# Linear attention and a Fourier mix on one core: loads as two streams, one pool of eight PSUM banks, the division in six operations, and a changed rank

## The chip, the cores and the metric

The kernel runs on one core of one Trainium2 chip. The metric is the device time of one execution in microseconds (us). Runs of the same kernel are compared on the same chip.

The core's engines run side by side, each in the order of its own instruction list. TensorE (PE; its weight loads are listed as PEld) multiplies matrices and transposes, and writes to PSUM, which has eight banks of 128 x 512 float32. VectorE (DVE) and ScalarE (ACT) read PSUM and compute elementwise. GpSimd (POOL) computes elementwise in SBUF, the on-chip memory, and issues the weights' DMAs. SyncE (SP) issues all other DMAs, in order: one that waits holds up those behind it.

## What is computed

The inputs are q, k and v of 8 batches x 8 heads x 576 rows x 64, a matrix omega of 128 x 64, and two weight matrices, 512 x 2048 and 2048 x 512. All is float32.

```python
q_s, k_s = (q * scale, k * scale)
def phi(x):
    proj = np.einsum('bhsd,md->bhsm', x, omega)
    sq = np.sum(x * x, axis=-1, keepdims=True) / 2.0
    h = proj - sq
    h = h - np.max(h, axis=-1, keepdims=True)
    return np.exp(h) / np.sqrt(m)
q_p, k_p = (phi(q_s), phi(k_s))
kv = np.einsum('bhsm,bhsd->bhmd', k_p, v)
z = np.sum(k_p, axis=2)
num = np.einsum('bhsm,bhmd->bhsd', q_p, kv)
den = np.einsum('bhsm,bhm->bhs', q_p, z)[..., None] + 1e-06
x = num / den                       # heads side by side: 8 x 576 x 512
...
X = np.fft.fft(x, axis=1)
X = np.fft.fft(X, axis=2)
u = x + np.real(X).astype(np.float32)
mu = np.mean(u, axis=-1, keepdims=True)
var = np.mean((u - mu) ** 2, axis=-1, keepdims=True)
un = (u - mu) / np.sqrt(var + 1e-06)
ch = np.maximum(un @ w_ch1, 0.0) @ w_ch2
return u + ch
```

## The kernel before

**Attention** goes over 32 pairs of heads, four to a batch. `loads()` (L241) fetches k and q of a pair into one kq tile (288 KB each, L248 and L251) and v into one of the fixed vd buffers (two DMAs of 144 KB, L254); vd has a column of ones per head, so that the product with it gives the sum z as well. `attn(n)` (L404) works on one pair: nine transposes of kq (tps, L368), evicted by ACT to kqT; products with omega (pp, L429), in five groups of at most 512 columns; the negated maximum on DVE (nmx, L384) and the exponential on ACT (e, L396); the product of k's features with vd (kvp, L451), kept by DVE as kv (L463); transposes of q's features (tps, L368) to qeT; and 18 products of qeT with kv, nine for each head (ndp, L493), into two banks. Each of these 18 gives 64 rows, and `SLOTS` (L28) says in which half of the partitions and in which of five slots of 65 columns a product lands. PE lists two instructions for each such product. The last step (L498 to L513) adds a small number to the denominators, inverts them and multiplies, and writes x: three DVE operations for each head on the four slots with 128 rows, and three on the fifth slot, which has 64 rows: twelve in all.

**Mixing** (`mix`, L520) works on a batch when its four pairs are done: folds on DVE, products with tables of cosines and sines on PE (yp L572, ab L599 and L604), and sums; u then goes to DRAM (us, uh). The tables are loaded within `loads()`, behind the second pair's v (L258).

**The weights** come as float64 (`weights`, L318): POOL loads 32 raw pieces of 512 KB into four slab buffers, and ACT, DVE and POOL narrow each to float32 (`narrow`, L297).

**The network behind it** has two forms. Four plain tiles of 128 rows (`plain_of`, L748: hp L780, evicted to ht; op L803; residual ur L816) are computed beside attention. The other 4096 rows come as eight blocks of 512, whose products are taken by halves (sx, sy, sz; L934 and L1024), after attention is over. A tile is normed by `norm_of` (L700): u is loaded from DRAM into one of two u buffers, normed on DVE (L709 to L715), transposed on PE (tp, L719) and evicted to unT. The first block's norms (`block_norms(0, mlpp)`, L832) are also listed beside attention, once all weights are narrowed; the four slab buffers then hold them.

**What sets the order.** No engine chooses its work while the kernel runs. Every piece of work is a `Step` with an engine, a cost, a due time `late` that is added to its end before others may use what it made, the events it needs (`after`), and the buffers it takes and gives back. `Listing.run` (L88) always takes, of the next steps of all streams, the one that could begin earliest; between equal ones that of the stream that stands earlier in the list goes first, and this is what rank means here. Each engine's list is written in this order. A `Step` is only a plan: what really waits on the chip is what its data and buffers demand.

The streams before stand in this order: `first`, `loads`, `frames` (which hands out the two x buffers), `plain_norms`, `mixing`, three streams `pairs` that each run every third pair, `plain`, `weights`, and the first block's norms. There are three kq buffers, two vd buffers, six PSUM banks for all of attention, mixing and norms (`bank`), and two that only the plain tiles use (`mm`).

Of the kernel before, what the change touches and what calls it, by code (L numbers as in the profile page):

```python
# [14 lines left out]
ALU = mybir.AluOpType  # L15
# [147 lines left out]
def kernel(  # L163
# [10 lines left out]
    nc = tc.nc  # L174
# [16 lines left out]
    R = S // 64  # L191

    NS = 3
    NV = 2
    NKQ = 3
    NE = 7


# [30 lines left out]
    buffers = dict(  # L229
        bank=6, mm=2, kq=NKQ, turned=NS, e=NE, e1=NS, kv=NS, x0=1, x1=1, fold=1, half=1, y=1,  # L230
        bmp=2, slab=4, u=2, unT=1, ht=NFC, ur=1, **{f"vd{i}": 1 for i in range(NV)},
    )

# [7 lines left out]
    def loads():  # L241
        for n in range(B * NP):
            b, pr = divmod(n, NP)
            h = slice(2 * pr, 2 * pr + 2)
            rows = "i (p r) d -> (i p) r d"
            yield Step(SP, 0.5, 3.0, take=("kq",))
            kq = ld.tile([P, 2 * R, D], F32, name="kq", tag="kq")
            nc.sync.dma_start(kq[:, 0:R, :], k[b, h].rearrange(rows, r=R))  # L248
            kqs[n] = kq
            yield Step(SP, 0.45, 4.0, makes=("kq", n))  # L250
            nc.sync.dma_start(kq[:, R : 2 * R, :], q[b, h].rearrange(rows, r=R))  # L251
            yield Step(SP, 1.3, 4.5, take=(f"vd{n % NV}",), makes=("vd", n))
            for i in range(2):
                nc.sync.dma_start(  # L254
                    vds[n % NV][D * i : D * i + D, :, (D + 1) * i : (D + 1) * i + D],
                    v[b, 2 * pr + i].rearrange("(p r) d -> p r d", r=R),
                )
# [145 lines left out]

    def attn(n):  # L404
        b, pr = divmod(n, NP)
        yield Step(NONE, after=(("kq", n), "om2"))
        kq = kqs.pop(n)

        flat = kq[:].rearrange("p c d -> p (c d)")
# [75 lines left out]
        )  # L485
        ndp = [bank("ndp"), bank("ndp")]

        for i, order in enumerate(((0, 2, 1, 4, 3, 7, 8, 5, 6), (2, 1, 4, 3, 7, 8, 5, 6, 0))):
            for r in order:
                g, slot = SLOTS[r]  # L490

                c0 = D * (1 - i if r >= 5 else i)
                nc.tensor.matmul(  # L493
                    ndp[i][D * g : D * g + D, (D + 1) * slot : (D + 1) * slot + D + 1],
                    lhsT=qeT[:, r, c0 : c0 + D],
                    rhs=kvs[0][:, i, :],
                )
        yield Step(DVE, 2.0, after=(("frame", b),), give=("bank", "bank"), makes=("x", b, pr))  # L498
        x = xts[b % 2]
        rden = small.tile([P, 2, 5], F32, name="rden", tag="rden")  # L500
        for i in range(2):
            nd = ndp[i][:, 0 : 5 * (D + 1)].rearrange("p (c d) -> p c d", d=D + 1)
            cols = slice((2 * pr + i) * D, (2 * pr + i + 1) * D)
            for p1, c0, c1 in ((P, 0, 4), (64, 4, 5)):
                den = rden[0:p1, i, c0:c1]
                nc.vector.tensor_scalar(den, nd[0:p1, c0:c1, D], DEN_EPS, None, op0=ALU.add)
                nc.vector.reciprocal(out=den, in_=den)
                nc.vector.tensor_tensor(
                    out=x[0:p1, c0:c1, cols],
                    in0=nd[0:p1, c0:c1, 0:D],  # L510
                    in1=den.unsqueeze(2).to_broadcast([p1, c1 - c0, D]),
                    op=ALU.mult,
                )  # L513

    def frames():
        for b in range(B):
# [231 lines left out]
    def plain_of(j):  # L748
# [4 lines left out]
        def hidden(fc, hp):  # L753
            step = Step(
                {ACT: 0.15 + TP / 1130.0, DVE: 0.15 + TP / 945.0},
                late=0.1,
                take=("ht",),
                give=("mm",),
                makes=("ht", key, fc),
            )  # L760
            yield step
            ht = mlpp.tile([128, TP], F32, name="ht", tag="ht", bufs=NFC)
            if step.eng == DVE:
                nc.vector.tensor_scalar(ht[:], hp[:, 0:TP], 0.0, None, op0=ALU.max)
            else:
                nc.scalar.activation(out=ht[:], in_=hp[:, 0:TP], func=AF.Relu)
            hs[fc] = ht

        for fc in range(NFC):
            yield Step(  # L770
                PE,
                8 * TP / 1193.0,
                after=tuple(("unT", key, i) for i in range(nt))
                + tuple(("w", fc * 128 // CV * NDC + dc) for dc in range(NDC)),
                take=("mm",),
                give=("unT",) if fc == NFC - 1 else (),
            )
            hp = mmp.tile([128, 512], F32, name="hp", tag="mm")
            for dc in range(NDC):
                nc.tensor.matmul(  # L780
                    hp[:, 0:TP],
                    lhsT=w1[:, dc, 128 * fc : 128 * fc + 128],
                    rhs=unTs[key][:, dc, :],
                    start=(dc == 0),
                    stop=(dc == NDC - 1),
                )
            yield Fork(hidden(fc, hp))
        for i in range(nt):
            for f0 in range(0, NFC, 2):
                yield Step(  # L790
                    PE,
                    1.72,
                    after=tuple(("ht", key, f) for f in (f0, f0 + 1))
                    + tuple(("w", NDC * DFF // CV + f) for f in (f0, f0 + 1)),
                    take=("mm",) if f0 == 0 else (),
                    give=("ht", "ht") if i == nt - 1 else (),
                    makes=("op", nt * j + i) if f0 == NFC - 2 else None,
                )
                if f0 == 0:
                    yp = mmp.tile([128, DM], F32, name="op", tag="mm")  # L800
                    yield Fork(rest(nt * j + i, yp))
                for fc in range(f0, f0 + 2):
                    nc.tensor.matmul(  # L803
                        yp[:],
                        lhsT=hs[fc][:, 128 * i : 128 * i + 128],
                        rhs=w2[:, fc, :],
                        start=(fc == 0),
                        stop=(fc == NFC - 1),
                    )

    def rest(t, yp):
        yield Step(SP, 0.5, 2.7, take=("ur",))
        ur = mlpp.tile([P, DM], F32, name="ur", tag="ur", bufs=1)
        load_rows(ur, t)
        yield Step(DVE, 0.7, after=(("op", t),), give=("mm",))
# [39 lines left out]
    def pairs(start):  # L855
# [268 lines left out]
```

## Time and profile before

| | us |
|---|---|
| median of three runs | 1384.61 |
| lowest and highest | 1383.97, 1388.35 |
| the profiled execution | 1387.42 |
| its span, first to last instruction | 1385.7 |

The profiled execution is 1.7 us longer than its span, and 2.8 us longer than the median. In the timelines a line gives the start, the length, the engine and line of the kernel, the operation, output and inputs, and in square brackets how long the engine had been idle before it and what ended that. The lists of waits give, for each pair of waiter and releaser, the total in us, the number of times, and the longest. A matmul's length is that of one instruction through the pipeline; several are under way at once, so what they cost is read from the distance of their starts.

### The profile page before, as it was taken

The numbers are of one execution on the slowest core, as the hardware profiler recorded it, in microseconds if no ns is written. First come the engines' busy times: TensorE is split into PE (matmuls) and PEld (weight loads), VectorE is DVE, ScalarE is ACT, GpSimd is POOL, SyncE is SP. The second block draws the span as 40 slices with busy tenths as digits, with TensorE's granted clock in tenths as the row PEclk, the third lists the DMA queues.
The fourth block names the chain that finished last, engine by engine and source line by source line (L and its number), as shares of the span: only waits on it lengthen the run. The fifth ranks groups of instructions, "written<-read, shape, count | busy, mean of one in ns | idle before, by whom it ended". The sixth has DMA issues, their size and how long they took to land.

```text
span 1385.7 us, 20262 instructions
## 1 busy us (share of the span) xinstructions
PE 1317.3 (95%) x7777; PEld 1137.5 (82%) x7777; DVE 586.7 (42%) x1545; ACT 409.1 (30%) x1194; POOL 291.8 (21%) x404
## 2 busy tenths in 40 slices
PE   6897989798999999889999999999999999999998
PEld 5777888676898786678888888888888888888887
DVE  2686878876666554155123123113123122132111
ACT  4664564555465451121021021020120120110210
POOL 1213123221100000034033042042140140330330
PEclk8999999999999999999999999999999999999999
DMA  7516155624422321110020100200200200200101
GB/s 193 153 43 192 53 169 169 173 90 114 124 78 77 79 88 37 37 54 16 14 63 16 46 31 16 76 1 16 76 0 16 76 7 13 73 16 8 54 1 31
DMA packets 82465, 89.67 MB, mean 65 GB/s; under 512 B 42944, under 2 KB 51392, under 8 KB 82368
## 3 DMA queue, kind: packets, MB, share of 16 engines
q1 hardware_dynamic: 77760, 71.59, 19.0%
q0 software_dynamic: 4608, 16.78, 3.7%
q8 instruction: 62, 1.02, 0.3%
q14 instruction: 35, 0.29, 0.1%
HBM read 69.47 MB, written 23.07 MB: 67 GB/s over the span
## 4 chain that ended last, share of the span: by engine, by line
PE 85%; DMA 6%; DVE 4%; SPq 2%; issue 1%; ACT 1%; POOL 1%; DVEq 0%; ACTq 0%; POOLq 0%
PE sx L1024 16%; PE sx L934 16%; PE sz L1024 8%; PE sz L934 8%; PE pp L429 7%; PE sy L1024 4%; PE hp L780 4%; PE sy L934 4%; PE yp L572 4%; PE op L803 4%; PE tps L368 3%; PE kvp L451 3%; PE ndp L493 2%; DMA kq<-in_q_dram 2%; PE ab L599 2%; DMA kq<-in_k_dram 2%
## 5 line engine op out<-in xcount | busy, mean ns | idle before, releaser
L396 ACT ACTIVATE e<-pp,nmx 128x128 f32<-128x128 f32 x576 | 156.7, 413 | 63.1 <-DVE nmx L384 61.6
L998 POOL TENSOR_TENSOR hs<-ht,ht 128x256 f32<-128x256 f32 x64 | 47.9, 750 | 488.5 <-DVE ht L921 488.5
L948 ACT ACTIVATE s<-sx 128x256 f32<-128x256 f32 x128 | 48.9, 383 | 344.0 <-PE sx L934 326.7
L429 PE MATMUL pp<-om,kqT 128*128 128x256 f32 x576 | 140.7, 391 | 1.1 <-ACT kqT L375 1.1
L934 PE MATMUL sx<-unT,w 128*128 128x256 f32 x512 | 131.2, 379 | 0.8 <-DVE ur L816 0.8
L429 PEld LDWEIGHTS pp<-om,kqT 128*128 128x128 f32 x576 | 108.7, 196 | 20.5 <-issue 2.0
L384 DVE TENSOR_REDUCE nmx<-pp 128x4 f32<-128x512 f32 (+1 forms) x160 | 96.0, 630 | 63.0 <-PE pp L429 59.1
L1024 PE MATMUL sx<-w,ht 128*128 128x256 f32 x512 | 114.4, 379 | 0.0
L934 PEld LDWEIGHTS sx<-unT,w 128*128 128x128 f32 x512 | 97.2, 190 | 14.8 <-DVE ur L816 1.6
L1024 PEld LDWEIGHTS sx<-w,ht 128*128 128x128 f32 x512 | 96.7, 190 | 12.9
L921 DVE CUSTOM_DVE_ANT_0 ht<-sz,s 128x256 f32<-128x256 f32 x64 | 27.1, 425 | 184.7 <-PE sz L934 184.7
L316 POOL TENSOR_TENSOR w<-w,raw 128x512 f32<-128x512 f32 x32 | 45.4, 1424 | 195.0 <-DVE raw L314 194.8
L1035 DVE TENSOR_TENSOR ur<-ur,sx 128x256 f32<-128x256 f32 x64 | 26.9, 421 | 139.8 <-PE sx L1024 139.8
L451 PE MATMUL kvp<-vd,e 128*128 128x130 f32 x576 | 75.3, 281 | 10.9 <-DMA vd<-in_v_dram 9.4
L451 PEld LDWEIGHTS kvp<-vd,e 128*128 128x128 f32 x576 | 71.7, 195 | 16.9 <-issue 10.8
L368 PE MATMUL tps<-ident,kq 128*128 128x128 f32 x288 | 49.1, 308 | 32.8 <-DMA kq<-in_k_dram 27.0
L981 ACT ACTIVATE ht<-sx 128x256 f32<-128x256 f32 x64 | 24.5, 383 | 172.3 <-PE sx L934 172.3
L368 PEld LDWEIGHTS tps<-ident,kq 128*128 128x128 f32 x288 | 37.3, 157 | 40.8 <-issue 28.8
L375 ACT ACTIVATE kqT<-tps 128x512 f32<-128x512 f32 (+1 forms) x96 | 43.7, 497 | 82.1 <-PE tps L368 81.8
L934 PE MATMUL sz<-tt,w1s 128*128 128x256 f32 x256 | 65.6, 379 | 1.9 <-DVE w1s L906 1.9
L934 PE MATMUL sx<-tt,w 128*128 128x256 f32 x256 | 65.6, 379 | 1.0 <-DVE ht L921 1.0
L934 PE MATMUL sz<-unT,w1s 128*128 128x256 f32 x256 | 65.5, 379 | 0.0
(105 smaller groups left out, 2329.5 us busy)
## 6 DMA issues: line engine op xcount, KB each, us to landing
raw<-in_moe_w_ch_dram POOLq DMA_DIRECT2D x32, 512.0 KB, 6.6
kq<-in_k_dram SPq DMA_DIRECT2D x32, 288.0 KB, 5.1
kq<-in_q_dram SPq DMA_DIRECT2D x32, 288.0 KB, 5.1
vd<-in_v_dram SPq DMA_DIRECT2D x64, 144.0 KB, 4.4
out_dram<-ur SPq DMA_DIRECT2D x72, 128.0 KB, 2.4
u<-us SPq DMA_DIRECT2D x32, 256.0 KB, 3.8
ur<-us SPq DMA_DIRECT2D x32, 256.0 KB, 3.6
uh<-x SPq DMA_DIRECT2D x16, 256.0 KB, 2.0
```

Of the source, the lines that this page charges most:

```text
L368: nc.tensor.transpose(ps[:, (j - j0) * 128 : (j - j0 + 1) * 128], src(j), ident[:])
L384: nc.vector.tensor_reduce(nmx[:, 0:num], ps[:, 0 : MF * num].rearrange("p (c m) -> p c m", m=MF), axis=AX.X, op=ALU.max, negate=True,)
L396: nc.scalar.activation(out=e[:, c, :], in_=ps[:, MF * c : MF * c + MF], func=AF.Exp, bias=nmx[:, c : c + 1],)
L429: nc.tensor.matmul(ps[:, 256 * j : 256 * j + 256], lhsT=kqT[:, 2 * t + j, :], rhs=om2[:].rearrange("p i m -> p (i m)"),)
L451: nc.tensor.matmul(kvp[:, 0 : 2 * (D + 1)], lhsT=feature(r), rhs=vds[n % NV][:, r, :], start=(r == 0), stop=(r == R - 1),)
L572: nc.tensor.matmul(yp[:, 0:NK], lhsT=fold[:, c, n, :], rhs=tab[:, c, :], start=(c == 0), stop=(c == NC3 - 1),)
L780: nc.tensor.matmul(hp[:, 0:TP], lhsT=w1[:, dc, 128 * fc : 128 * fc + 128], rhs=unTs[key][:, dc, :], start=(dc == 0), stop=(dc == NDC - 1),)
L803: nc.tensor.matmul(yp[:], lhsT=hs[fc][:, 128 * i : 128 * i + 128], rhs=w2[:, fc, :], start=(fc == 0), stop=(fc == NFC - 1),)
L934: nc.tensor.matmul(ps[:, 0:HT], lhsT=left(dc), rhs=right(dc), start=start and dc == 0, stop=(dc == D2 - 1), skip_group_check=True,)
L948: nc.scalar.activation(out=s[:], in_=ps[:, 0:HT], func=AF.Copy)
L998: nc.gpsimd.tensor_tensor(out=o, in0=l, in1=r, op=op)
L1024: nc.tensor.matmul(ps[:, 0:HM], lhsT=left(fc), rhs=right(fc), start=start and fc == 0, stop=(fc == HF - 1), skip_group_check=True,)
```

## The change

- The loads become two streams. `loads()` keeps k and q, with due times of 5.0 and 5.5 us, and the tables behind the second q; the new `loads_v()` stands right behind it in the list and has v. There are three vd buffers instead of two, and two kq buffers instead of three.
- A pair's stream now also waits, in the plan, for the v of the pair before.
- The pools of six and two PSUM banks become one of eight, from which the plain tiles take too.
- The products for r = 0 leave their slots: for each head one product with a stationary operand of 128 columns instead of 64 is written to a slot of its own in the second bank (only its first 64 rows are used), so that this bank holds six slots and the first four. The last step on DVE is then two additions, one inversion of all ten columns, and three multiplications. Its planned cost is 1.8 us instead of 2.0.
- The first block's norms stand ahead of `plain` and `weights` in the list of streams.

```diff
-    NV = 2
-    NKQ = 3
+    NV = 3
+    NKQ = 2
...
-    psum = early.enter_context(tc.tile_pool(name="psum", bufs=6, space=PSUM))
-    mmp = early.enter_context(tc.tile_pool(name="mmp", bufs=2, space=PSUM))
+    psum = early.enter_context(tc.tile_pool(name="psum", bufs=8, space=PSUM))
...
-            yield Step(SP, 0.5, 3.0, take=("kq",))
+            yield Step(SP, 0.6, 5.0, take=("kq",))
...
-            yield Step(SP, 0.45, 4.0, makes=("kq", n))
+            yield Step(SP, 0.45, 5.5, makes=("kq", n))
             nc.sync.dma_start(kq[:, R : 2 * R, :], q[b, h].rearrange(rows, r=R))
-            yield Step(SP, 1.3, 4.5, take=(f"vd{n % NV}",), makes=("vd", n))
+            if n == 1:
+                yield from load_tables()
+
+    def loads_v():
+        for n in range(B * NP):
+            b, pr = divmod(n, NP)
+            yield Step(SP, 1.3, 5.5, take=(f"vd{n % NV}",), makes=("vd", n))
             for i in range(2):
...
-            if n == 1:
-                yield from load_tables()
...
-        yield Step(NONE, after=(("kq", n), "om2"))
+        yield Step(NONE, after=(("kq", n), "om2") + ((("vd", n - 1),) if n else ()))
...
-        for i, order in enumerate(((0, 2, 1, 4, 3, 7, 8, 5, 6), (2, 1, 4, 3, 7, 8, 5, 6, 0))):
+        for i, order in enumerate(((2, 1, 4, 3, 7, 8, 5, 6), (2, 1, 4, 3, 7, 8, 5, 6))):
...
+        flat = qeT[:].rearrange("q c p -> q (c p)")
+        for i in range(2):
+            nc.tensor.matmul(
+                ndp[1][:, (D + 1) * (4 + i) : (D + 1) * (5 + i)],
+                lhsT=flat[:, D * i : D * i + P],
+                rhs=kvs[0][:, i, :],
+            )
...
-        for i in range(2):
-            nd = ndp[i][:, 0 : 5 * (D + 1)].rearrange("p (c d) -> p c d", d=D + 1)
-            cols = slice((2 * pr + i) * D, (2 * pr + i + 1) * D)
-            for p1, c0, c1 in ((P, 0, 4), (64, 4, 5)):
-                den = rden[0:p1, i, c0:c1]
-                nc.vector.tensor_scalar(den, nd[0:p1, c0:c1, D], DEN_EPS, None, op0=ALU.add)
-                nc.vector.reciprocal(out=den, in_=den)
-                nc.vector.tensor_tensor(
...
+        for i, n in enumerate((4, 6)):
+            nc.vector.tensor_scalar(
+                rden[:, 4 * i : 4 * i + n], nds[i][:, :, D], DEN_EPS, None, op0=ALU.add
+            )
+        nc.vector.reciprocal(out=rden[:], in_=rden[:])
+        cols = x[:, :, 2 * D * pr : 2 * D * (pr + 1)].rearrange("p c (i d) -> p c i d", i=2)
+        for p1, dst, nd, den in (
+            (P, cols[:, 0:4, 0], nds[0], rden[:, 0:4]),
+            (P, cols[:, 0:4, 1], nds[1][:, 0:4], rden[:, 4:8]),
+            (64, cols[0:64, 4], nds[1][0:64, 4:6], rden[0:64, 8:10]),
+        ):
+            nc.vector.tensor_tensor(
...
-            hp = mmp.tile([128, 512], F32, name="hp", tag="mm")
+            hp = bank("hp")
...
-                    yp = mmp.tile([128, DM], F32, name="op", tag="mm")
+                    yp = bank("op")
...
-        [first(), loads(), frames(), plain_norms(), mixing()]
+        [first(), loads(), loads_v(), frames(), plain_norms(), mixing()]
         + [pairs(i) for i in range(NS)]
-        + [plain(), weights(), block_norms(0, mlpp)]
+        + [block_norms(0, mlpp), plain(), weights()]
```

More of the change, by code (lines that the diff above doesn't have):

```diff
@@ L497, in attn @@
                 )
-        yield Step(DVE, 2.0, after=(("frame", b),), give=("bank", "bank"), makes=("x", b, pr))
-        x = xts[b % 2]
-        rden = small.tile([P, 2, 5], F32, name="rden", tag="rden")
-        for i in range(2):
-            nd = ndp[i][:, 0 : 5 * (D + 1)].rearrange("p (c d) -> p c d", d=D + 1)
-            cols = slice((2 * pr + i) * D, (2 * pr + i + 1) * D)
-            for p1, c0, c1 in ((P, 0, 4), (64, 4, 5)):
-                den = rden[0:p1, i, c0:c1]
[L506 to L513, printed above, removed]
+        flat = qeT[:].rearrange("q c p -> q (c p)")
[5 more added lines that the diff above has]
+            )
+        yield Step(DVE, 1.8, after=(("frame", b),), give=("bank", "bank"), makes=("x", b, pr))
+        x = xts[b % 2]
+        rden = small.tile([P, 10], F32, name="rden", tag="rden")
+        nds = [
+            t[:, 0 : (D + 1) * n].rearrange("p (c d) -> p c d", d=D + 1)
+            for t, n in zip(ndp, (4, 6))
+        ]
+        for i, n in enumerate((4, 6)):
[10 more added lines that the diff above has]
+            nc.vector.tensor_tensor(
+                out=dst,
+                in0=nd[:, :, 0:D],
+                in1=den.unsqueeze(2).to_broadcast(list(dst.shape)),
+                op=ALU.mult,
+            )
     def frames():
@@ L757, in hidden @@
                 take=("ht",),
-                give=("mm",),
+                give=("bank",),
                 makes=("ht", key, fc),
@@ L774, in plain_of @@
                 + tuple(("w", fc * 128 // CV * NDC + dc) for dc in range(NDC)),
[L775 removed]
+                take=("bank",),
                 give=("unT",) if fc == NFC - 1 else (),
             )
[L778 removed]
+            hp = bank("hp")
             for dc in range(NDC):
@@ L794, in plain_of @@
                     + tuple(("w", NDC * DFF // CV + f) for f in (f0, f0 + 1)),
-                    take=("mm",) if f0 == 0 else (),
+                    take=("bank",) if f0 == 0 else (),
                     give=("ht", "ht") if i == nt - 1 else (),
@@ L814, in rest @@
         load_rows(ur, t)
-        yield Step(DVE, 0.7, after=(("op", t),), give=("mm",))
+        yield Step(DVE, 0.7, after=(("op", t),), give=("bank",))
         nc.vector.tensor_tensor(out=ur[:], in0=ur[:], in1=yp[:], op=ALU.add)
```

6 lines of the change are left out of this document (3 added, 3 removed).

## The prediction

> **What bounds the kernel now.** I read the page's busy line first, then the span cut in two where the halved blocks begin, then TensorE's waits.
>
> ```profile
> PE 1317.3 (95%) x7777; PEld 1137.5 (82%) x7777; DVE 586.7 (42%) x1545; ACT 409.1 (30%) x1194; POOL 291.8 (21%) x404
> ```
>
> ```profile
> 0.00:591.48 591.48, 530.68 (x4082) 445.89 (x4082) 377.40 (x1069) 294.44 (x910) 94.94 (x120) 0.97 0.39 109
> 591.48:1385.70 794.22, 786.61 (x3696) 691.64 (x3696) 209.34 (x476) 114.66 (x284) 196.91 (x284) 1.00 0.12 31
> ```
>
> The columns of the second view are the stretch, its length, and the busy time of PE, PEld, DVE, ACT and POOL; then the granted clock, the DMA share and GB/s. In the halved blocks PE stands for 7.6 us, so nothing is to be had there, and the change does not touch their instructions. In the first 591 us it stands for 60.8 us, and the clock averages 0.97. PE is the bound there too, so a gain must come out of those 60.8 us, the clock, or PE's work. What PE waits for:
>
> ```profile
> PE tps L368 <- DMA kq<-in_k_dram: 27.0, 8, 8.6
> PE kvp L451 <- DMA vd<-in_v_dram: 9.4, 4, 5.2
> PE tp L719 <- DVE u L715: 5.7, 1, 5.7
> ```
>
> Loads make 36.4 of the 60.8 us. One of them in time, on SP's queue and on PE:
>
> ```profile
> 60.35 0.97 SPq L248 DMA_DIRECT2D kq<-in_k_dram  x1
> 61.37 0.43 SPq L251 DMA_DIRECT2D kq<-in_q_dram  x1
> 63.43 1.55 SPq L254 DMA_DIRECT2D vd<-in_v_dram  x2
> 65.03 0.65 SPq L248 DMA_DIRECT2D kq<-in_k_dram  x1
> 65.72 0.43 SPq L251 DMA_DIRECT2D kq<-in_q_dram  x1
> 108.22 1.22 SPq L254 DMA_DIRECT2D vd<-in_v_dram  x2
> ```
>
> ```profile
> 63.24 0.71 PE L368 MATMUL tps<-ident,e 128*128 128x128 f32 x5
> 68.28 0.63 PE L368 MATMUL tps<-ident,kq 128*128 128x128 f32 x4 [4.33 <-DMA kq<-in_k_dram]
> ...
> 325.27 2.16 PE L368 MATMUL tps<-ident,kq 128*128 128x128 f32 x9 [2.40 <-DMA kq<-in_k_dram]
> ```
>
> ```profile
> DMA to landing us min/median/max: 3.2/5.1/9.7
> ```
>
> A pair's v waits for one of two vd buffers, at 108.22 for 42 us, and the next pair's k and q stand behind it in the one list of `loads()`. When the buffers come free, three pairs' loads leave together and PE, which runs in order, reaches the transposes of k before k has landed (the last row: the 32 loads of k, median 5.1, longest 9.7 us). Each such stand costs twice, since the granted clock then drops:
>
> ```profile
> 69.80:73.20 3.40, 3.38 (x14) 3.16 (x15) 0.00 (x0) 1.96 (x5) 0.00 (x0) 0.57 0.26 74
> ...
> 325.80:329.20 3.40, 3.40 (x44) 2.89 (x42) 0.39 (x3) 1.36 (x3) 0.00 (x0) 0.57 0.81 264
> sum 20.40, PE 19.02 PEld 17.69 DVE 6.26 ACT 11.79 POOL 4.12; mean PE 3.80 PEld 3.54 DVE 1.25 ACT 2.36 POOL 0.82
> ```
>
> These are the first and last of five stretches behind load waits, with their sum: 19.02 us of PE at a clock of 0.54 to 0.57, so about 0.45 of it, 8.6 us, is lost.
>
> The Trainium skill, TensorE: Matmul & The Clock Gate, Part 1, says that the array falls to half rate after an idle window of about 3.4 us. The row at 325.27 shows a wait of 2.40 us with the clock at 0.57 right behind it, so here shorter waits cost clock as well; by the page's rule alone such short waits cost no clock, the 2.2 us of clock that I leave over below would go as well, and the time would be 1358.
>
> **The change part by part.**
>
> *Loads in two streams.* k and q no longer stand behind v: with two kq buffers they leave when the pair two ahead has been transposed, and v, with three, when the kvp three ahead is done. In the code the due times become 5.0 and 5.5 us for k and q instead of 3.0 and 4.0, near the measured median of 5.1, and a pair starts only when the v before its own is due; so the written order puts other PE work where PE now stands. At stake after the start: 27.0 - 8.6 (the longest, at 23.83, taken with the start below) = 18.4, plus 9.4 for v = 27.8 us, and 8.6 of clock. Bounds: all of it goes (-36.4) or none. Loads up to 9.7 us remain longer than their due times, so I take three quarters: -20.9 and -6.4. The added waits sit in SP's one queue: behind a k that waits for transposes stand stores of us and out, loads of u and ur, and v. Those are the price if PE is late, and are the rivals below.
>
> *The start.* The tables are yielded inside `loads()` behind the second q, so they now go ahead of the first v.
>
> ```profile
> 6.58 1.26 SPq L291 DMA_DIRECT2D cs_sb<-k_cs  x2
> ...
> 16.00 2.89 SPq L291 DMA_DIRECT2D sd_sb<-k_sd  x2
> 20.02 0.35 SPq L248 DMA_DIRECT2D kq<-in_k_dram  x1
> ```
>
> ```profile
> 11.12 2.17 PE L451 MATMUL kvp<-vd,e 128*128 128x130 f32 x18
> ...
> 14.66 0.60 PE L368 MATMUL tps<-ident,e 128*128 128x128 f32 x4
> 23.83 1.09 PE L368 MATMUL tps<-ident,kq 128*128 128x128 f32 x4 [8.57 <-DMA kq<-in_k_dram]
> ```
>
> What follows the tables in the queue now, the third k, lands at 23.8. The first v takes that place less the v loads that no longer precede it, so at 20 to 24 instead of before 11.1: PE stands about 11 us from 11.1 instead of 8.6 us from 15.3. Behind it the first two pairs' work covers the third k. Cost 2.5 us; bounds -5 (the v lands by 15) to +6.
>
> *Eight banks in one pool.* No row shows PE waiting for a bank by name. It lets attention use two more banks, and lets the plain tiles take more than two. I take nothing, bounds -5 to +6.
>
> *The first block's norms rank higher.* Now they go last:
>
> ```profile
> 505.48 0.54 DVE L715 TENSOR_SCALAR u<-u,mv,rstd 128x512 f32<-128x512 f32 x1
> ```
>
> ```profile
> 552.20 1.04 PE L719 MATMUL tp<-ident,u 128*128 128x128 f32 x8
> 558.92 1.11 PE L719 MATMUL tp<-ident,u 128*128 128x128 f32 x4 [5.68 <-DVE u L715]
> ```
>
> ```profile
> 557.90:564.70 6.80, 5.09 (x24) 4.69 (x25) 0.55 (x1) 1.08 (x3) 0.39 (x1) 0.53 0.33 100
> ```
>
> A normed u is ready at 506 and is transposed at 552; it holds a u buffer, and the last plain tile's norm can only begin then, so PE stands 5.7 us and then works 5.09 us at 0.53 (2.4 lost). Ranked ahead of the plain tiles the transposes come early and that buffer is free. -8.1, bounds -8.1 to 0.
>
> *The last step, on DVE.* Twelve operations become six.
>
> ```profile
> L506 DVE TENSOR_SCALAR rden<-ndp x128: 140/143/163, 30.0 to 522.6; 128x4 f32<-128x4 f32 x64, 64x1 f32<-64x1 f32 x64
> L507 DVE RECIPROCAL rden<-rden x128: 154/168/181, 30.2 to 522.8; 128x4 f32<-128x4 f32 x64, 64x1 f32<-64x1 f32 x64
> L508 DVE TENSOR_TENSOR x<-ndp,rden x128: 216/321/426, 30.4 to 523.0; 128x256 f32<-128x256 f32 x64, 64x64 f32<-64x64 f32 x64
> ```
>
> Before, 4 x (0.143 + 0.168 + 0.321) = 2.53 us a pair. After, 2 x 0.143 + 0.168 + three products, two of 0.426 and one of 64x128 between 0.216 and 0.426: 1.6 to 1.7. About 0.85 a pair, 27 us over 32 pairs, but DVE is busy for 377 of 591 us and PE covers it. I take nothing; bounds -7 (a quarter reaches the path) to 0.
>
> *The same step, on PE.* It keeps its 36 instructions a pair (two for each product), but the four for r = 0 now use the array's whole width instead of half of it.
>
> ```profile
> 45.66 2.55 PE L493 MATMUL ndp<-kv,qeT 128*64 128x65 f32 x72
> 48.14 0.70 PE L429 MATMUL pp<-om,kqT 128*128 128x256 f32 x2
> ```
>
> ```profile
> 102.48 0.73 PE L604 MATMUL ab<-mid,cs_sb 128*128 128x1 f32 x6
> 103.07 0.69 PE L599 MATMUL ab<-cd_sb,y 128*128 128x129 f32 x4
> ```
>
> Half-width ones start (48.14 - 45.66) / 72 = 34 ns apart, whole ones with hardly any columns (103.07 - 102.48) / 6 = 98 ns. 4 x 0.064 x 32 = +8.2 us of PE work. Bounds 0 to 8.2; I take the upper, as PE is the bound and 98 ns is the nearest row.
>
> The Trainium skill, TensorEngine Tiling (Array Packing), Key Properties, says that tiles of a split array load and multiply in parallel; that speaks against this part. By it a whole-width product costs what two packed ones cost, +0.034 each, 4.4 us in all, and the sum would be 3.8 lower; the rows say 98 against 34, so I keep 8.2.
>
> **Sum**, against the profiled execution's 1387.4 (span 1385.7): +2.5 - 20.9 - 6.4 - 8.1 + 8.2 = -24.7, so 1362.7. That execution lies 2.8 above the median of 1384.6, so 1360.
>
> **The rivals.**
>
> *The wait moves (0.19).* Two streams are still one in-order queue: if a k stands behind a v or a store as often as now, the 18.4 us stay with their share of the clock (5.7). Only v's part goes: +2.5 - 7.1 - 2.2 - 8.1 + 8.2 = -6.7, that is 1378. For it: SP's order is written from due times that the long loads exceed. Against it: a k needs only transposes, which come first in a pair, where now it needs a v buffer, which comes free late.
>
> *Two kq buffers are too few (0.14), slower.* Three pairs run at once, so of each three the last's k can leave only when the first's transposes are done. If the three are transposed in a row, PE does the second's nine (four took 0.63, so about 1.3 us) and stands for the rest of a landing between 5.1 and 9.7, say 7.4 - 1.3 = 6.1, with 1.7 of clock (8.6 over five stretches): 7.8 for each of ten such groups. Seven of ten make 54.6 against the 36.4 that go: +18.2 + 2.5 - 8.1 + 8.2 = +20.8, or 1405. It decides from (36.4 - 2.6) / 7.8, about five groups of ten. Against it: the due times now carry 5.0 us, so the list would have to be wrong by some 2 us each time.
>
> *DVE was on the path (0.10).* Then 7 us more go: 1353.
>
> **How the numbers follow.** The forecast holds 0.57 and spans 1345 to 1376 by its own bounds. Measurement tells some 0.3% (4 us) from no change: faster is all of the forecast but 0.02, DVE's 0.10 and half of the moved wait (0.10), 0.75; the rest of the moved wait and of the forecast is 0.11; slower 0.14. Down, all of the load waits, clock and tail go and the start gains 5: 1338. Up, the range takes in the moved wait and the near end of the slower rival: 1390.
>
> **What would show it.** Loads: the waits of tps on k after 30 us under 8 us, and the clock at 1.0 through the stretches above. Start: kvp at 20 to 24 with about 11 us idle before it, on v. Norms: the block's transposes before 500 and no 5.7 us wait near the end. PE: the whole-width products 90 to 100 ns apart. Most of the gain must lie before the first halved block, which should begin some 25 us earlier. Wrong would be: the k waits of the same size at other places, waits of pp on banks that a plain tile holds, or halved blocks that take other than 794 us.

## The result, and the profile after

The change took the median from 1386.09 to 1330.17 us; the ratio is 0.960, with a 95% interval of 0.958 to 0.963. That is 56 us, where 25 were forecast, and below the range. The profiled execution took 1329.8 us, 57.7 less than the one before. The first product of the halved blocks starts at 533.95 instead of 591.48 us, so all of it lies ahead of them. First the stretches up to and from there, in the view by windows with the columns of before:

```profile
0.00:533.95 533.95, 516.00 (x4081) 443.14 (x4081) 348.95 (x871) 292.43 (x916) 97.57 (x123) 0.99 0.43 121
533.95:1328.00 794.05, 786.62 (x3696) 692.13 (x3696) 209.16 (x476) 114.67 (x284) 196.71 (x284) 1.00 0.12 31
```

The halved blocks are what they were (794 us). Before them PE stands for 18.0 us instead of 60.8, and it is busy for 14.7 us less. Cut once more, at 40 us, behind the start; first the kernel before, then the change:

```profile
0.00:40.00 40.00, 27.16 (x176) 23.76 (x177) 14.18 (x36) 21.62 (x65) 6.56 (x20) 0.87 0.69 183
40.00:591.48 551.48, 503.52 (x3908) 422.13 (x3906) 363.22 (x1034) 272.82 (x846) 88.39 (x100) 0.97 0.36 104
```

```profile
0.00:40.00 40.00, 26.11 (x163) 23.13 (x164) 15.32 (x33) 20.51 (x62) 9.66 (x25) 0.87 0.83 217
40.00:533.95 493.95, 489.88 (x3920) 420.01 (x3918) 333.64 (x839) 271.93 (x856) 87.92 (x98) 1.00 0.40 113
```

After the first 40 us PE's idle time fell from 48.0 to 4.1 us and its busy time by 13.6 us, with the granted clock at 1.00 instead of 0.97. The waits of PE in the change up to 600 us, as the list of waits has them (the rows of L953 lie in the first halved block):

```profile
PE kvp L455 <- DMA vd<-in_v_dram: 9.8, 1, 9.8
PE omps L348 <- DMA om<-in_omega_dram: 3.3, 1, 3.3
PE yp L591 <- DVE fold L566: 3.0, 3, 1.9
PE sz L953 <- DVE w1s L925: 1.8, 1, 1.8
PE sx L953 <- DVE ht L940: 1.0, 1, 1.0
PE sx L953 <- DVE ur L835: 0.8, 1, 0.8
PE tps L371 <- DMA kq<-in_k_dram: 0.7, 1, 0.7
```

No wait for k is left but the 0.7 us before the very first transposes, and the wait for a normed u is gone. The one large wait, for v, is that of the start, on PE's and on SP's line in time:

```profile
6.76 4.92 PE L433 MATMUL pp<-om,kqT 128*128 128x256 f32 x18
21.50 4.23 PE L455 MATMUL kvp<-vd,e 128*128 128x130 f32 x18 [9.82 <-DMA vd<-in_v_dram]
...
28.49 1.15 PE L496 MATMUL ndp<-kv,qeT 128*64 128x65 f32 x32
29.57 0.66 PE L504 MATMUL ndp<-kv,qeT 128*128 128x65 f32 x4
30.07 1.30 PE L433 MATMUL pp<-om,kqT 128*128 128x256 f32 x5
```

```profile
7.33 1.81 SPq L294 DMA_DIRECT2D sd_sb<-k_sd  x2
10.36 5.59 SPq L259 DMA_DIRECT2D vd<-in_v_dram  x4
```

The v loads leave behind the tables and kvp begins at 21.5 us, as forecast. The last three lines of PE give the price of the whole-width products: (30.07 - 29.57) / 4 = 0.125 us apart, beside (29.57 - 28.49) / 32 = 0.034 for half-width ones.

### The profile page after: what moved, and what is told of

Same layout as the page of the kernel before. It is cut to its first block, busy times and chain, and to the rows that moved or that the text cites. A ratio compares the mean times of both kernels' runs of the same rounds, so it can differ in the third digit from the quotient of the medians.

```text
span 1328.0 us, 20075 instructions
## 1 busy us (share of the span) xinstructions
PE 1302.6 (98%) x7777; PEld 1135.3 (85%) x7777; DVE 558.1 (42%) x1347; ACT 407.1 (31%) x1200; POOL 294.3 (22%) x407
## 4 chain that ended last, share of the span: by engine, by line
PE 95%; DMA 2%; DVE 2%; SPq 1%; issue 0%; ACT 0%; DVEq 0%
PE sx L1043 17%; PE sx L953 16%; PE pp L433 8%; PE sz L1043 8%; PE sz L953 8%; PE kvp L455 5%; PE tps L371 4%; PE sy L1043 4%; PE sy L953 4%; PE op L822 4%; PE hp L799 4%; PE yp L591 4%; PE ndp L496 3%; PE ab L618 2%; PE ndp L504 1%; PE tp L738 1%
## 5 line engine op out<-in xcount | busy, mean ns | idle before, releaser
L433 PE MATMUL pp<-om,kqT 128*128 128x256 f32 x576 | 136.3, 382 | 0.0
L953 PE MATMUL sx<-unT,w 128*128 128x256 f32 x512 | 131.2, 379 | 0.8 <-DVE ur L835 0.8
L433 PEld LDWEIGHTS pp<-om,kqT 128*128 128x128 f32 x576 | 106.0, 192 | 14.4 <-issue 1.2
L953 PEld LDWEIGHTS sx<-unT,w 128*128 128x128 f32 x512 | 97.2, 190 | 14.7 <-DVE ur L835 1.6
L387 DVE TENSOR_REDUCE nmx<-pp 128x4 f32<-128x512 f32 (+1 forms) x160 | 95.9, 629 | 28.5 <-PE pp L433 20.7
L1043 PEld LDWEIGHTS sx<-w,ht 128*128 128x128 f32 x512 | 96.8, 190 | 12.8
L953 PE MATMUL sz<-tt,w1s 128*128 128x256 f32 x256 | 65.6, 379 | 1.8 <-DVE w1s L925 1.8
L953 PE MATMUL sx<-tt,w 128*128 128x256 f32 x256 | 65.7, 380 | 1.0 <-DVE ht L940 1.0
L953 PE MATMUL sz<-unT,w1s 128*128 128x256 f32 x256 | 65.6, 379 | 0.0
L953 PE MATMUL sx<-tt,w1s 128*128 128x256 f32 x256 | 65.6, 379 | 0.0
L953 PE MATMUL sy<-unT,w 128*128 128x256 f32 x256 | 65.6, 379 | 0.0
L378 ACT ACTIVATE qeT<-tps 128x512 f32<-128x512 f32 (+1 forms) x96 | 44.9, 497 | 54.7 <-PE tps L371 54.4
```

The costliest lines, as they stand in the source:

```text
L387: nc.vector.tensor_reduce(nmx[:, 0:num], ps[:, 0 : MF * num].rearrange("p (c m) -> p c m", m=MF), axis=AX.X, op=ALU.max, negate=True,)
L433: nc.tensor.matmul(ps[:, 256 * j : 256 * j + 256], lhsT=kqT[:, 2 * t + j, :], rhs=om2[:].rearrange("p i m -> p (i m)"),)
L953: nc.tensor.matmul(ps[:, 0:HT], lhsT=left(dc), rhs=right(dc), start=start and dc == 0, stop=(dc == D2 - 1), skip_group_check=True,)
L1043: nc.tensor.matmul(ps[:, 0:HM], lhsT=left(fc), rhs=right(fc), start=start and fc == 0, stop=(fc == HF - 1), skip_group_check=True,)
```

## The experiments

The change has four parts: the loads (L), the rank of the first block's norms (R), the pool of eight banks (P), and the division with its products (D). In the tables below, before is the kernel before in the same series of runs. Its median was 1386.1 us beside the change and lay between 1386.5 and 1388.5 in the later series, so medians from different series carry some 2 us of this, and where a difference is small the ratio is what to compare.

### One part put back

Three theories: the loads carry the gain; the banks give the plan other work for every gap; or DVE's relief opened the path.

```diff
 (L put back)
-        [first(), loads(), loads_v(), frames(), plain_norms(), mixing()]
+        [first(), loads(), frames(), plain_norms(), mixing()]
-    NV = 3
-    NKQ = 2
+    NV = 2
+    NKQ = 3
... (with the old loads(), due times and start of a pair)
 (P put back)
-    psum = early.enter_context(tc.tile_pool(name="psum", bufs=8, space=PSUM))
+    psum = early.enter_context(tc.tile_pool(name="psum", bufs=6, space=PSUM))
+    mmp = early.enter_context(tc.tile_pool(name="mmp", bufs=2, space=PSUM))
... (with the plan's two counts of banks, and the plain tiles on the second pool)
 (D put back)
-        for i, order in enumerate(((2, 1, 4, 3, 7, 8, 5, 6), (2, 1, 4, 3, 7, 8, 5, 6))):
+        for i, order in enumerate(((0, 2, 1, 4, 3, 7, 8, 5, 6), (2, 1, 4, 3, 7, 8, 5, 6, 0))):
... (with the twelve operations and their planned cost of 2.0)
 (R put back)
-        + [block_norms(0, mlpp), plain(), weights()]
+        + [plain(), weights(), block_norms(0, mlpp)]
```

> The change with its loads put back as they were: one stream, three kq and two vd buffers, the old due times, no wait for the v of the pair before. Theory 1, the loads carry the whole gain after the start (48.0 us of idle PE after 40 us became 4.1): PE's waits on k and v come back with the clock behind them, 36 us or more, and the start gains some 2: 1365 to 1382. Theory 2, eight banks give the plan other work for every gap, and the loads are worth only the 27 us that were forecast less what the cover saves: 1345 to 1358, and few k waits of over 3 us. Theory 3, the six DVE operations opened the path: 1345 or less.

> The change with PSUM split into six and two banks again. Theory 1 (loads alone): 1328 to 1334. Theory 2 (the banks are the part that was missed): some 20 us of the idle time come back as small waits of PE on ACT and DVE, 1345 to 1355. Theory 3: 1328 to 1334.

> The change with the last step as it was, twelve DVE operations and r = 0 in half-width products. The four whole-width products start 0.123 us apart in the trace of the change ((30.07 - 29.57) / 4) against 0.034 for half-width ones, so 0.36 us a pair, 11 us over 32 pairs, of PE work go. Theories 1 and 2: PE is the bound at 97% busy in this part, so the time falls to 1317 to 1323. Theory 3 (DVE's relief carries the gain): it rises by 5 to 25, 1335 to 1355.

> The change with the first block's norms last in the list again. As forecast, the wait of 5.7 us for the last plain tile's norm and 2.4 us of clock come back: 1336 to 1340. Rival: with more banks and less waiting the norms find their place anyway, and the rank is worth nothing: 1328 to 1332.

| put back | median, us | ratio to before, 95% interval |
|---|---|---|
| nothing (the change) | 1330.2 | 0.960 (0.958 to 0.963) |
| L | 1385.4 | 0.999 (0.997 to 1.001) |
| P | 1340.7 | 0.967 (0.966 to 0.969) |
| D | 1332.8 | 0.962 (0.960 to 0.964) |
| R | 1343.6 | 0.969 (0.968 to 0.971) |

All four lie outside every range that was given: the first above theory 1's 1365 to 1382, P and D between the ranges of their theories, R above 1336 to 1340. Without the loads nothing is left of the gain that is clear of the noise: R, P and D together take 9.7 us off PE's idle time after 40 us then, and PE's work rises by 6.6 us (510.1 instead of 503.5). But with the loads in place each of P and R is worth over 10 us, so the loads alone cannot be worth 56 either. The waits of PE after 40 us in the run with L put back:

```profile
PE tps L367 <- DMA kq<-in_k_dram: 17.4, 7, 4.0
PE kvp L451 <- DMA vd<-in_v_dram: 5.2, 3, 4.4
PE tps L367 <- DMA kq<-in_q_dram: 4.7, 4, 2.1
```

These are 27.3 us of load waits, about as many as the same three rows have after 40 us in the kernel before (17.5, 9.4 and 1.6, together 28.5). The run with R put back has these:

```profile
PE tp L738 <- DVE u L734: 7.3, 2, 5.7
PE yp L591 <- DVE fold L566: 3.0, 3, 1.9
PE hp L799 <- ACT unT L742: 1.4, 2, 0.7
```

The 5.7 us wait for the last plain tile's norm is back, with a second one. The rank was expected at 6 to 10 us and is worth 13. With D put back PE saves the whole-width products, yet the time rises by 2.6 us, where theories 1 and 2 had it fall by 7 or more. PE's longest wait in that run after 40 us is one of 5.6 us for a normed u, at 243 us. DVE had itself stood 6.1 us there for the load of that u, so this wait is one for a load, and it is not shown that a less busy DVE is what took it away.

### The loads alone, the start, and half-width products

The first of these is the kernel before with L only. The others start from the change: the tables behind the second v; r = 0 in half-width products in the same two slots, with a third addition of 64 rows (seven DVE operations); and both. In the half-width kernels the inverted denominators also get two fixed tiles, set to 1.0 at the start, as the inversion covers rows that no addition writes.

```diff
 (tables)
     def loads():
...
-            if n == 1:
-                yield from load_tables()
     def loads_v():
...
+            if n == 1:
+                yield from load_tables()
 (half width)
-        for i, order in enumerate(((2, 1, 4, 3, 7, 8, 5, 6), (2, 1, 4, 3, 7, 8, 5, 6))):
+        for i, order in enumerate(((0, 2, 1, 4, 3, 7, 8, 5, 6), (2, 1, 4, 3, 7, 8, 5, 6, 0))):
             for r in order:
-                g, slot = SLOTS[r]
+                g, slot = SLOTS[r] if r else (0, 4 + i)
...
-                    ndp[i][
+                    ndp[i if r else 1][
...
-        for i, n in enumerate((4, 6)):
+        for p1, i, c0, c1 in ((P, 0, 0, 4), (P, 1, 0, 4), (64, 1, 4, 6)):
```

> The kernel before with only the loads changed (two streams, three vd and two kq buffers, the new due times, the wait for the v of the pair before). Theory A: the loads' own term was about right (forecast -24.8 with the start), and the 30 us that were missed come from banks, rank and division, which pay only once PE no longer waits for loads: 1352 to 1364. Theory B: the loads alone free nearly everything: 1330 to 1345. Putting the three other parts back one at a time cost 10.5, 13.4 and 2.6 us, 26.5 together, which speaks for A.

> The change with the four tables loaded behind the second v instead of behind the second q. If the 9.8 us in which the first kvp waits for v (to 21.5 us) are the price of that order, that wait goes; what is left is the third k behind the tables, as before. Gain 2 to 9 us: 1321 to 1328. Rival: DMA is full in the first 20 us (0.94 of its time), so the wait only moves from v to k: 1328 to 1332.

> The change with r = 0 in two half-width products again, in the same two slots of the second bank, and seven DVE operations instead of six (the third addition has 64 rows). If whole-width products cost what the trace shows (0.123 against 0.034 us, four a pair) and DVE's relief stays, 11 us go: 1317 to 1322. If PE's list absorbs them: 1328 to 1332. That the twelve operations with half-width products were 2.6 us slower than the change would then be 11 of PE less 14 of DVE.

> Both of the two edits before together. If they are independent, their gains add: 1308 to 1320.

| kernel | median, us | ratio to before, 95% interval |
|---|---|---|
| before with L alone | 1366.0 | 0.985 (0.982 to 0.987) |
| change, tables behind v | 1334.2 | 0.961 (0.959 to 0.964) |
| change, half-width r = 0 | 1323.3 | 0.954 (0.951 to 0.957) |
| change, both | 1328.1 | 0.956 (0.953 to 0.960) |

The loads alone give 21.5 us. The time lies 2 us above theory A's range and 21 above theory B's, so it speaks for A. The load waits are gone (the list of PE's waits after 40 us, with L alone), but others stand there:

```profile
PE tp L723 <- DVE u L719: 9.4, 2, 5.7
PE yp L576 <- ACT e L400: 8.7, 2, 7.6
PE yp L576 <- DVE fold L551: 2.8, 2, 2.5
PE yp L576 <- ACT unT L727: 1.4, 2, 0.7
```

The longest of the second row, in time, on DVE, ACT and PE:

```profile
120.44 0.69 DVE L713 BATCH_NORM_STATS2 st<-u 128x6 f32<-128x512 f32 x1 [4.89 <-DMA u<-us]
...
122.13 0.68 DVE L388 TENSOR_REDUCE nmx<-pp 128x4 f32<-128x512 f32 x1
122.73 1.01 DVE L551 TENSOR_TENSOR fold<-half 128x384 f32<-128x384 f32 x2
```

```profile
122.84 1.14 ACT L400 ACTIVATE e<-pp,nmx 128x128 f32<-128x128 f32 x4 [7.59 <-DVE nmx L388]
```

```profile
124.03 1.44 PE L576 MATMUL yp<-cs_sb,fold 128*128 128x320 f32 x2 [7.60 <-ACT e L400]
```

The yp product reads nothing of the exponential, so what the named wait stands for can only be the PSUM bank that the exponential empties. But the bank is not what cost the 7.6 us. The product reads fold, and DVE writes fold right behind the maximum, from 122.73 to 123.74; the exponential ends at 123.98 and comes last by 0.24 us. A load of u that is late holds DVE for 4.9 us, and the maximum, the exponential and fold all come late behind it. With L and P together (run below) the same product starts 0.70 us after its fold, which would be 123.43 here; so by this estimate the bank cost at most 0.6 of the 7.6 us. In that run the load of u leaves at 107.63 instead of 115.41 us, DVE stands 1.0 us for it, and the product starts without a wait:

```profile
115.00 1.27 PE L455 MATMUL kvp<-vd,e 128*128 128x130 f32 x8 [1.12 <-ACT e L399]
116.10 0.61 PE L723 MATMUL tp<-ident,u 128*128 128x128 f32 x4
116.62 3.47 PE L576 MATMUL yp<-cs_sb,fold 128*128 128x320 f32 x12
```

So at this place what the pool changes is the order in which the work is written. Banks are a buffer of the plan too: with six, a step that finds none is written later, and no engine need wait for it on the chip. Waits for a bank on the chip are there too, but shorter. In the run with P put back these products with omega wait 1.25 us for an exponential that they do not read:

```profile
52.22 2.60 PE L434 MATMUL pp<-om,kqT 128*128 128x256 f32 x10 [1.25 <-ACT e L400]
```

The tables behind v gain 2.2 us of PE work in the first 40 us (28.30 busy instead of 26.11) and lose 6 afterwards (500.0 instead of 493.95 us), where the instructions are the same and their order is not. The 9.8 us for v are gone, but PE now stands 7.5 us until 23.3 for k, so for the most part the wait only moved, as the rival had it; at 1334.2 the run lies above both ranges. Half-width products give 6.9 us, just short of the range that was given and less than the 11.6 that their distances promise (4 x 0.091 x 32; the expectations wrote 0.123 for 0.50 / 4, which is 0.125). This kernel is the fastest so far. With both edits the time is 1328.1, well above 1308 to 1320: the tables cost 4.8 us there, as they cost 4.0 alone, and half width gains 6.1.

### The loads' pieces, and the luck of the list

Each starts from the change: the old due times of the loads; three kq and two vd buffers; no wait, in the plan, for the v of the pair before; and two kernels in which one planned cost is altered and nothing else, the second of which ran with the next group.

```diff
 (due times)
-            yield Step(SP, 0.6, 5.0, take=("kq",))
+            yield Step(SP, 0.5, 3.0, take=("kq",))
-            yield Step(SP, 0.45, 5.5, makes=("kq", n))
+            yield Step(SP, 0.45, 4.0, makes=("kq", n))
-            yield Step(SP, 1.3, 5.5, take=(f"vd{n % NV}",), makes=("vd", n))
+            yield Step(SP, 1.3, 4.5, take=(f"vd{n % NV}",), makes=("vd", n))
 (buffers)
-    NV = 3
-    NKQ = 2
+    NV = 2
+    NKQ = 3
 (no planned wait)
-        yield Step(NONE, after=(("kq", n), "om2") + ((("vd", n - 1),) if n else ()))
+        yield Step(NONE, after=(("kq", n), "om2"))
 (first altered cost, of the ndp step)
             PE,
-            1.5,
+            1.55,
 (second altered cost)
-        yield Step(DVE, 0.15 + 0.135 * num)
+        yield Step(DVE, 0.16 + 0.135 * num)
```

> The change with the old due times and costs of the loads (3.0, 4.0 and 4.5 us), streams and buffers as changed. Theory D, the due times carry the loads' part: the list again reaches the transposes before k has landed, k waits of 10 to 25 us come back, 1345 to 1365. Theory B, the buffers carry it: k leaves early enough whatever the list expects, 1328 to 1336.

> The change with three kq and two vd buffers, as before, two streams and new due times kept. Theory B: v waits for its buffer as before and kvp waits for v, 1345 to 1380. Theory D: the list knows it and gives PE other work, 1328 to 1340.

> The change without the planned wait for the v of the pair before. It only shapes the list: if it keeps pairs from starting too far ahead of v, kvp waits for v come back, 1334 to 1345; if the buffers do that anyway, 1328 to 1334.

> The change with one number of the plan altered, the planned cost of the ndp step 1.55 instead of 1.5 us; no instruction, buffer or transfer is added or taken away, but the greedy list comes out another way. It measures how far the list alone moves the time. If the differences of 2.6 to 13 us between the runs so far are those of the parts, it stays within 3 us of the change, 1327 to 1333. If the list's luck is as large, it lies 4 to 12 us off, most likely above.

> The change with another number of the plan altered, the fixed part of the planned cost of the maximum on DVE 0.16 instead of 0.15 us; nothing physical changes. With the first such run (2.2 us under the change) it bounds the list's luck: within 4 us, 1326 to 1334, or more, up to 10.

| kernel | median, us | ratio to before, 95% interval |
|---|---|---|
| change, old due times | 1354.9 | 0.977 (0.974 to 0.979) |
| change, three kq, two vd | 1353.9 | 0.976 (0.973 to 0.978) |
| change, no planned wait | 1346.3 | 0.970 (0.967 to 0.973) |
| change, first altered cost | 1327.9 | 0.958 (0.955 to 0.960) |
| change, second altered cost | 1334.1 | 0.960 (0.958 to 0.963) |

Due times and buffers are both needed, each is worth 24 us beside the other, and neither theory holds alone. With the old due times it is k that is late, with the old buffers it is v (first row of PE's waits after 40 us in each of the two runs):

```profile
PE tps L371 <- DMA kq<-in_k_dram: 13.2, 2, 9.0
```

```profile
PE kvp L455 <- DMA vd<-in_v_dram: 10.9, 2, 7.0
```

The planned wait is worth 16 us although no data asks for it: without it kvp waits four times for v after 40 us, 6.7 us in all, as expected, and the time lies just over the 1334 to 1345 that were given. The two altered costs lie 2.2 us under and 3.9 us over the change by their medians, and 3.6 under and 0.4 over by their ratios to before. That much is the luck of the list together with the spread between series, and differences of up to 4 us between such kernels say nothing of their parts. The 2.6 us of D put back and the 4 us of the tables are among them.

### The parts added to the loads, and half width once more

Each of the first three is the kernel before with the loads and one other part; the edits are those shown. The last is the change with half-width products in another list, as the planned cost of that step is 1.3 instead of 1.5 us.

```diff
 (before, L and R)
-        + [plain(), weights(), block_norms(0, mlpp)]
+        + [block_norms(0, mlpp), plain(), weights()]
 (before, L and P)
-    psum = early.enter_context(tc.tile_pool(name="psum", bufs=6, space=PSUM))
-    mmp = early.enter_context(tc.tile_pool(name="mmp", bufs=2, space=PSUM))
+    psum = early.enter_context(tc.tile_pool(name="psum", bufs=8, space=PSUM))
... (with the plan's count of banks, and the plain tiles on this pool)
 (before, L and D)
-        for i, order in enumerate(((0, 2, 1, 4, 3, 7, 8, 5, 6), (2, 1, 4, 3, 7, 8, 5, 6, 0))):
+        for i, order in enumerate(((2, 1, 4, 3, 7, 8, 5, 6), (2, 1, 4, 3, 7, 8, 5, 6))):
... (with the whole-width products, the six operations and their planned cost)
 (half width, another list)
             PE,
-            1.5,
+            1.3,
```

> The kernel before with the loads and the rank changed. Theory A1, each part takes away a wait of its own: the two waits for a normed u (9.4 us in the loads-only run) and their clock go, 1352 to 1358. Theory A2, the parts need each other (a freed gap is filled by the next wait): less than half of that, 1359 to 1366.

> The kernel before with the loads and the pool changed. Theory A1: the waits of yp on banks that ACT frees (8.7 us) and the small ones go, 1350 to 1358. Theory A2: 1359 to 1366, the waits for u grow.

> The kernel before with the loads and the division changed. If the division's gain on DVE (14 us, from 11 of PE work less 2.6 measured) is there without the pool and the rank: 1360 to 1366, 3 us under the loads alone. If it is only worth something when PE waits for nothing else: 1366 to 1378, as 7 to 11 us of PE work come on top.

> The change with half-width products for r = 0 and seven DVE operations, as in the run that was 6.9 us under the change, and the planned cost of that PE step at 1.3 instead of 1.5 us (36 half-width instructions at 34 ns take 1.25). Same instructions, another list. If the 7 us are PE's work, it stays 5 us or more under the change: 1316 to 1326. If they were the list's luck (the two runs with one planned number altered lay 2.3 under and 3.9 over the change): anywhere from 1324 to 1336.

| parts | median, us | idle PE from 40 us to the halved blocks, us |
|---|---|---|
| none (before) | 1386 to 1389 | 48.0 |
| R, P, D without L | 1385.4 | 38.3 |
| L | 1366.0 | 31.9 |
| L, D | 1357.8 | 21.2 |
| L, R | 1349.2 | 20.8 |
| L, P | 1343.1 | 16.7 |
| L, P, D (R put back) | 1343.6 | 12.8 |
| L, R, D (P put back) | 1340.7 | 9.8 |
| L, R, P (D put back) | 1332.8 | 8.8 |
| all (the change) | 1330.2 | 4.1 |
| all, half-width r = 0 | 1323.3, and 1322.8 in another list | 6.3 in the first |

The last column is the window's length less PE's busy time in it, as for the change above. The pool gives 10.5 to 22.9 us according to what else is there, the rank 10.3 to 17.1, and the division between 8.4 less and 0.5 more. Beside the loads alone each part does more than was expected: P 1343.1 instead of 1350 to 1358, R 1349.2 instead of 1352 to 1358, D 1357.8 instead of 1360 to 1366. That speaks for A1, but the three do not add up: singly they give 22.9, 16.8 and 8.1 us, 47.8 in all, and together 35.8, so some of what each takes away is shared. The first row of PE's waits after 40 us in the run with L and P, and in that with L and R:

```profile
PE tp L723 <- DVE u L719: 12.6, 2, 7.3
```

```profile
PE yp L576 <- ACT e L400: 8.8, 2, 7.8
```

With the pool the wait of yp is gone and the waits for a normed u stay; with the rank it is the other way round. (The expectation of P puts the 8.7 us of yp to banks; by the rows above nearly all of it is the late fold.) That half-width products are 7 us faster holds in the second list too, at 1322.8 (ratio 0.953, 0.950 to 0.955), and PE is busy for 485.7 and 484.0 us after 40 us in these two instead of 489.9 in the change. Both lie below all three lists with whole-width products (1327.9 to 1334.1). So this is in the main PE's work and not luck, though its size is known to a few us only. These two kernels beat both the kernel before and the change.

## Why the prediction was wrong

**The direction, the place and the mechanism of the loads were right.** k and v no longer wait for each other, the waits of tps on k are gone, and the clock with them. The two loads terms and the start made -24.8; the loads alone measured -21.5, and by the interval of their ratio 18 to 25. All load waits after 40 us went in that trace, and not three quarters; part of that was given back in the waits behind a late load of u.

**The start** came out as said: kvp at 21.5 after 9.8 us idle, where "20 to 24" and "about 11" were forecast. Its price of 2.5 was about 1 (26.11 instead of 27.16 us of PE work by 40 us).

**The step that failed is "Eight banks in one pool ... I take nothing, bounds -5 to +6".** It rested on "No row shows PE waiting for a bank by name". In these traces such a wait carries the name of the engine that empties the bank, as the 1.25 us above, so no row would have the word; but even read rightly these waits are short, and of the 7.6 us of yp at most 0.6 was the bank. What the step left out is that banks are a buffer of the plan. The pool was worth 10.5 to 22.9 us, and at the place looked at the gain came by another written order, with an earlier load of u and other work for PE. That all of it comes this way is not shown.

**The rank was mis-sized** at -8.1: 10 to 17 us. Where only the rank is missing, and with the loads alone, there are two waits for a normed u (7.3 and 9.4 us, not 5.7 in one), and with the rank those are gone. It does not take away every such wait: the 5.6 us of the run with D put back stand beside the new rank.

**The division's sign was wrong.** On PE the whole-width products cost 0.125 us where 0.098 was taken, 11.6 us by distance against the forecast's 8.2, and some 7 by the time of the two half-width runs. The DVE time itself was right (busy 377 to 349 us, 28 where 27 were forecast). But of it nothing was taken, with -7 as the bound, and with the same half-width products, seven operations instead of twelve gave 9.5 us (1332.8 to 1323.3). So that a DVE busy for 64% of a stretch is covered does not follow from the share. How much of the 9.5 us is DVE's time and how much another list, made from another planned cost, is not shown: the one long wait that went with it was for a load.

**The clock was mis-sized.** I counted five stretches and one at the tail, 11.0 us. The whole part at 0.97 for 551 us is about 16 us, by a clock that the view gives to two places, and in the change that view has 1.00. This and small waits between instructions are the candidates for the fall in busy time, and the two are not separated: the same 288 transposes of k and q and the same 576 instructions of pp took 10.9 and 4.4 us less. Kernel before, then the change, groups of the page and of the list by lines:

```profile
L429 PE MATMUL pp<-om,kqT 128*128 128x256 f32 x576 | 140.7, 391 | 1.1 <-ACT kqT L375 1.1
...
L368 PE MATMUL tps<-ident,kq 128*128 128x128 f32 x288 | 49.1, 308 | 32.8 <-DMA kq<-in_k_dram 27.0
```

```profile
L433 PE MATMUL pp<-om,kqT 128*128 128x256 f32 x576 | 136.3, 382 | 0.0
...
L371 PE MATMUL tps<-ident,kq 128*128 128x128 f32 x288 | 38.2, 278 | 0.8 <-DMA kq<-in_k_dram 0.7
```

**The sum.** After 40 us the forecast took 26.6 us off idle time (20.9 and the 5.7 of the tail) and 0.6 off busy time (6.4 + 2.4 - 8.2); the trace has 43.9 and 13.6. So 17.3 us of the miss are idle time: 6.9 the quarter of the load waits that was left over, and 10.4 waits of other parts that I priced at nothing. Another 13.0 are PE's busy time, the clock and small waits, although the whole-width products cost more by their distances than forecast. The low end of the range, 1338, comes out only with the pool's bound of -5 added to what its sentence names (without it 1343), and it leaves out the bounds of the division on DVE (-7) and on PE (0). With these the terms' own bounds reach down to 1323 and take in the measured time, but pool and rank each lie outside their own bounds, so that would have been luck.

The rival that two kq buffers would be too few did not come about: k needs only transposes, as argued against it, and its landing fell from a median of 5.1 to one of 2.9 us (the change, the list of DMA issues):

```profile
kq<-in_k_dram SPq DMA_DIRECT2D x32, 288.0 KB, 2.9
```

What stays open is how much of each difference under 4 us is the list and not the part, and by which waits the pool and the division gain the whole of what they gain.

## What to carry to other kernels

Removing the load waits was worth 21 us alone, and it made three other edits, worth nothing without it, worth 36 us more. So before a part is priced at nothing, ask which wait stands there once the large one is gone, and whether the part changes what the plan can write and not only what the chip must wait for. A wait is put down to what came last: look up when the instruction's own operands were written before it is blamed on a bank. Where a list is made by a greedy plan, alter one planned cost by a few per cent and see how far the time moves before differences of that size are given a cause.

## What was not expected of the hardware

A whole-width product of 65 columns starts every 0.125 us beside 0.034 for a half-width one, more than the three or so times that the rows of before suggested. The inversion of ten columns takes 0.216 us where those of four columns and of one took 0.168 in the median. The third is the clock: in the kernel before PE stood 1.29 us until 319.64 and 2.40 us until 325.27, and the clock was 1.00 up to 325.2 us and then 0.57 for 3.4 us, so waits as short as these can cost clock.
